# Weight preparation on estimated time: rests between a transfer and its first reader counted in estimated microseconds instead of scheduler ticks, an earlier and partly VectorE-made second gate chunk

## The chip, the cores and the metric

One core of one Trainium2 chip runs the whole program in one launch. The metric is the device time of an execution in microseconds (us). TensorE is called PE, VectorE DVE, ScalarE ACT, GpSimd POOL, and SP is the engine whose queue issues most of the DMA transfers.

## The reference, cut to what matters

```python
x = A_x                                     # (1, 2048, 576), f32
xn = _layernorm(x)
qkv = (xn @ wqkv).reshape(B, S, 3, 32, 18)  # 32 heads of 18
p = softmax(einsum("bhqd,bhkd->bhqk", q, k) * 18 ** -0.5)
s = einsum("bhqk,bhkd->bhqd", p, v) ... @ wo
h = gelu(xn @ w_gate) * (xn @ w_up)         # 576 -> 4608
g = silu(h @ w_down)                        # 4608 -> 576
return x + s * g
```

## The kernel before, in words

Every f32 matrix product is made of f16 products: a matrix is scaled by a power of two and split into a high and a low f16 half, and three of the four products of halves are added up in PSUM. The normed input is split once (`XHT`, `XL`). The weights are split while the program runs, in *chunks*: the projection groups `j0` to `j4` (seven heads' query and key columns each), the value weights `v`, eighteen gate/up/down chunks `c0` to `c17` of 256 hidden columns each, and `wo`. The order is v, j1, c0, c1, j2, c2, c3, j3, c4, c5, j4, c6, ... c17, wo.

`prep` (L195) makes the list of pieces by which one chunk is prepared. The **load** issues the DMAs of the raw weights: two for the gate, two for the up columns (L215, L219), and for a `c` chunk one for the rows of `w_down` (L227). There is one raw buffer and one down buffer, so a load waits on SP until POOL has read the chunk before to its end. Then DVE takes the **absolute maximum** of the five 128-row tiles (L234) and of the two down tiles (L239), and of these (`par`, L248, L251); a column of 128 maxima goes out to DRAM (L260, tile `mxd`), comes back spread over all partitions (`spread`, L275, tile `mb`), and DVE reduces it (`top`, L281, tile `mg`) and makes scale factors of it (L286 to L298, tiles `E` and `s`). ACT then writes the five **high halves** (L316), and POOL the five **low halves** in two instructions each (L323, L324); `fin` marks the chunk as ready. The halves of the down rows follow, and `dfin`.

These pieces lie in one queue, `bg`. The program that records the instructions calls `subtick` once per step of its main loops; each call is a **tick**, with a budget of time on ACT, DVE and, through `"T"`, on POOL. A tick records up to three pieces (six in a tick that closes a pair of gate products) while the budget lasts. An empty piece `(None, None)` ends the tick: a **rest** of n such pieces makes the queue wait n ticks. Rests stand ahead of the load (`lead`), between the load and the first maximum, between `par` and `spread`, between `spread` and `top`, and ahead of the high halves. A tick has no fixed length on the chip. In the first attention loop (pair 0, L1440 on) two ticks go with each pair of score tiles, in the main loop (L1560 on) one tick goes with each score tile and its share of other work.

Each engine runs its own instructions in the order of recording, so a piece recorded early stands ahead of all that its engine records later, and where it has to wait, the rest of that engine's work waits too. The other DVE work: the maximum of each tile of scores (`PM`, L1235), which frees the PSUM buffer that PE needs two score tiles later; a one-element copy `touch` (L422), after which PE begins the second half of a pair of gate products (`Pair`, L454); the sums `osb` of the products with V (L1331, L1333) after each burst of them (L1325), `y` (L764), and the small steps at the end of a head pair (`max_end`, L1245 to L1254).

The norm of an attention output goes through DRAM as well, in steps that are put off by a number of ticks (`norm`, `chained`): `sd`, `oc` (L1361), the reciprocal (L1364), `rd` (L1368), the spread denominators `obr` (L1372, 256 KB), and four ticks later the product on DVE (L1375). These DMAs, the loads of Q, K and V tiles, the stores of projected Q and K (L520) and the chunk loads all go through SP, in one order.

A chunk must be ready when its first product is recorded (`unit_w`, `until`). `start_prep` (L964) queues chunk i + 1 and i + 2 when unit i begins.

Of the kernel before, what the change touches and what calls it, by code (L numbers as in the profile page):

```python
# [33 lines left out]
FIRST = {"A": 0.75, "V": 0.75, "T": 1.3}  # L34
FREE = {"A": 4.0, "V": 4.0, "T": 1.3}
# [6 lines left out]
class Deferred:  # L42
# [4 lines left out]
    def __init__(self):  # L47
        self.now = 0
        self.items = []
        self.n = 0  # L50
        self.room = {}
        self.pool = 0.0

    def at(self, when, fn, cost=None):
        self.items.append((max(when, self.now + 1), self.n, fn, cost))
        self.n += 1
# [13 lines left out]
    def advance(self, room):  # L70
        self.now += 1
        self.room = dict(room)
        self.pool = max(0.0, self.pool - room["T"])
        while True:
            due = [i for i in self.items if i[0] <= self.now and self.fits(i[3])]
            if not due:
                return
            i = min(due, key=lambda i: i[:2])
            self.items.remove(i)
            self.spend(i[3])  # L80
            i[2]()


def on_act(t=0.7):
    return {"A": t}


def on_dve(t=0.7):
    return {"V": t}


def on_pool(t):
    return {"G": t}
# [3 lines left out]
def kernel(ctx: ExitStack, tc: tile.TileContext, x, wqkv, wo, w_gate, w_up, w_down, out):  # L97
# [11 lines left out]
    class Stage:  # L109

        def __init__(self):
            self.sb = self.pt = None
# [18 lines left out]
    defer = Deferred()  # L131
    bg = deque()
# [5 lines left out]
            self.open = open  # L138


    def subtick(room=FREE, most=3):
        defer.advance(room)
        n = 0
        while bg and n < most:
            if isinstance(bg[0], Gate):
                if not bg[0].open():
                    return
                bg.popleft()
                continue
            cost, fn = bg[0]  # L150
            if not defer.fits(cost):
                return
            defer.spend(cost)
            bg.popleft()
            n += 1
            if fn is None:
                return
            fn()
# [33 lines left out]
    class W:  # L192
        pass

    def prep(name, parts, n, down=None, urgent=False, free=None, dfree=None, lead=1, slow=0):  # L195


        w = W()
        w.ready = w.dready = False
        w.n = n  # L200
        pieces = []
        gap = 0 if urgent else 1
        q = nc.sync
        npart = len(parts)

# [106 lines left out]
        def split_hi(t):  # L312
            if t == 0:
                w.hi = wp.tile([P, 5, 2, n], F16, tag="whi", name=f"whi_{name}")
                w.lo = wp.tile([P, 5, 2, n], F16, tag="wlo", name=f"wlo_{name}")
            nc.scalar.activation(w.hi[:, t], w.raw[:, t], AF.Copy, scale=w.s[:, 0:1])  # L316

        def low(lo, raw, sc, hi):

            if urgent:  # L320
                nc.vector.scalar_tensor_tensor(lo, raw, sc, hi, op0=ALU.mult, op1=ALU.subtract)
            else:
                nc.gpsimd.tensor_scalar(raw, raw, sc, None, op0=ALU.mult)  # L323
                nc.gpsimd.tensor_tensor(lo, raw, hi, op=ALU.subtract)  # L324

        def split_lo(t):
            low(w.lo[:, t], w.raw[:, t], w.s[:, 0:1], w.hi[:, t])

        def dsplit_hi(t):
            if t == 0:  # L330
# [13 lines left out]
        def add(fn, cost=None):  # L344
            pieces.append((cost, fn))

        def rest(n):
            for _ in range(n * gap):
                pieces.append((None, None))

        act, dve = on_act(), on_dve()
        low_cost = dve if urgent else on_pool(2.75)
        pieces += [(None, None)] * (lead * gap)
        add(load)
        rest(5 + slow)
        for t in range(5):
            add(lambda t=t: amax(t), dve)
        if down is not None:
# [2 lines left out]
        add(par, dve)  # L361
        if urgent:
            add(par2)
        rest(3)
        add(spread)
        rest(4)
        add(top, on_dve(0.4))
        for fn in (power, floor, inverse):
            add(fn, on_dve(0.2))
        rest(1)  # L370
        if free is not None:
            pieces.append(Gate(free))
        for t in range(5):
            add(lambda t=t: split_hi(t), act)
            if t:
                add(lambda t=t: split_lo(t - 1), low_cost)
        add(lambda: split_lo(4), low_cost)
        if down is not None:
            add(units, on_dve(0.2))
            add(back, on_dve(0.3))  # L380
# [181 lines left out]
    def spec_j(j):  # L562
        n = DH * len(heads_of(j))
        return f"j{j}", [(wqkv, 126 * j), (wqkv, D + 126 * j)], n
# [400 lines left out]
    def start_prep(i):  # L965
        if i < len(order) and i not in preps:
            kind, spec = order[i]
            w, pieces = prep(
                *spec, free=lambda: done_units[0] >= i - 1,
                dfree=lambda: kind[1] < 2 or dndone[kind[1] - 2] == NT,  # L970
                lead=8 if i == 3 else 1, slow=2 if i == 2 else 0,
            )
            preps[i] = w
            bg.extend(pieces)
            if kind == "wo":
                bg.extend(begin_wo(w))
# [77 lines left out]

    def fills(n, amt):
        for _ in range(n):
            subtick()
            fill(amt)


    w0, p0 = prep(*spec_j(0), urgent=True)
# [82 lines left out]
    with tc.manual_schedule():  # L1144
        for t in range(4):
            load_x(t, 1, nc.scalar)
        p0[0][1]()
        for t in range(4, NT, 4):
            load_x(t, 4, nc.sync)
        nc.vector.memset(epst, EPS)  # L1150
        pw = [f for _, f in p0[1:] if f is not None]
        s0, s1 = ln_stats(0, 2), ln_stats(2, 2)
        for f in s0:
            f()
        ln_norm(0)
        ln_norm(1)
        for f in s1[:3] + pw[:5]:
            f()
        ln_tr(0)
        ln_out(0)  # L1160
        for f in pw[5:6] + s1[3:7] + pw[6:12] + s1[7:]:
            f()
        ln_norm(2)
        pw[12]()
        ln_tr(1)
        ln_out(1)
        for f in pw[13:]:
            f()
        lnq = deque()
        for t in range(4, NT, 4):  # L1170
            lnq.extend(ln_stats(t, 4))
        for _ in range(12):
            lnq.popleft()()
        for it in range(2, NT + 2):
            g, i = divmod(it, 4)
            if 2 < it < NT:
                ln_norm(it)
            if g < 3:
                for _ in range((0, 0, 0, 5)[it] if it < 4 else (5, 4, 4, 4)[i]):
                    if lnq:  # L1180
                        lnq.popleft()()
            if it == 5:
                open_j(w0, 0)
            if it == 5:
                preps[0], pieces = prep(*order[0][1], urgent=True)
                pv0 = deque(f for _, f in pieces if f is not None)
                pv0.popleft()()
            for _ in range(V_PLAN.get(it, 0)):
                pv0.popleft()()
            if it == 2:  # L1190
                proj_fine(0)
            if it > 2:
                if it - 1 < NT:
                    ln_tr(it - 1)
                if it - 2 > 1:
                    ln_out(it - 2)
                subtick()
                proj_fine(it - 2)
        while pv0:
            pv0.popleft()()  # L1200
        start_prep(1)
        start_prep(2)
        for _ in range(3):
            subtick()
# [226 lines left out]
    filler[0] = unit_v(preps[0])  # L1431
    load_qk(0)
    fills(9, 2.0)
    k = 0
    while k < 64:
# [23 lines left out]
    for k in range(5):  # L1459
        if k in (0, 1, 3):  # L1460
            steps[k - k // 3]()
        g_run(14)
        if k:
            qk1(1, next(items))
        subtick(FIRST)
    assert mdone.get(0)

    def last_gen():
# [93 lines left out]
    for p in range(NPAIR - 1):  # L1562
        if p not in VT:
            load_v(p)
        for i in range(4 * NT):
# [22 lines left out]
            step = plan.popleft() if plan else None  # L1588
            late = False
# [9 lines left out]
            if d and not behind:  # L1599
                if dn is None:  # L1600
                    dn = DownPair()
                late = dn.run()
            if gs.closed:
                gs.closed = False
                if late:
                    dn.evac()
                    dn = None
                subtick({"A": 2.2, "V": 1.4 if late else 2.2, "T": 0.7 + 0.86 * len(pend) + 0.73 * d}, 6)
                flush(("ma", "mb") if d else ("md", "ma"))
                summed = not d  # L1610
            else:
                subtick({"A": 0.75, "V": 0.0 if late or step is not None and step[2] < 1.45 and len(bg) < 70 else 0.75, "T": 2.0 if step is None else 0.45 + step[2]})
                if late:
                    dn.evac()
                    dn = None
                g_run(7 if step is None else step[1])
                if behind:
                    dn = DownPair()
                    dn.run()
# [20 lines left out]
    for i in range(4 * NT):  # L1640
# [17 lines left out]
        if phase >= 2:  # L1658
            nphase = 0
            n = next((k + 1 for k, u in enumerate(pend) if u[2] == NT - 1), len(pend))  # L1660
# [61 lines left out]
```

## Time and profile before

| what | value |
| --- | --- |
| median of 3 runs | 2635.53 us (2624.99 to 2636.22) |
| the profiled execution | 2634.51 us |
| its span, from the first to the last instruction | 2632.7 us |
| mean granted PE clock | 0.989 |
| busy of the span | PE 96%, DVE 73%, ACT 63%, POOL 57% |

A row of the timeline reads: start, length, engine, line, operation, output<-inputs, shapes, count, and in brackets how long the engine sat idle before it and what ended that. A row of SP is the issue of a DMA, not its transfer. A row of the table of windows reads: stretch, its length, busy time and count for PE, for PE's weight loads, DVE, ACT and POOL, then the granted PE clock, the busy share of the DMA engines, and GB/s.

### The profile page before, as it was taken

How to read it: one execution, taken by the hardware profiler on the slowest of the kernel's cores; microseconds unless marked ns; L12 is line 12 of the kernel's file. 1: busy time of each engine (PE TensorE's matmuls, PEld its weight loads, DVE VectorE, ACT ScalarE, POOL GpSimd, SP SyncE). 2: the span in 40 equal slices, each digit the busy share in tenths (PEclk: the TensorE clock that was granted, in tenths of full speed). 3: DMA queues.
4: the chain of work that ended last, by engine and by line, in shares of the span. 5: the costliest groups of instructions: out<-in, count | busy, mean ns of one | idle time of the engine just before them, and what ended most of it. 6: DMA issues, size and time to landing. Idle time of an engine off the chain costs nothing.

```text
span 2632.7 us, 59553 instructions
## 1 busy us (share of the span) xinstructions
PE 2534.8 (96%) x25220; PEld 1317.2 (50%) x25220; DVE 1927.1 (73%) x2712; ACT 1664.6 (63%) x2083; POOL 1492.3 (57%) x1422
## 2 busy tenths in 40 slices
PE   6889999899999999999999999999999999999898
PEld 5554545345545454454544555455455554555344
DVE  7576778777777778777877777777777777777444
ACT  5225666666767666767666676677666666766563
POOL 4237653575527544758475675756566666747301
PEclk9999999999999999999999999999999999999999
DMA  4430022202030012112011111202010111100123
GB/s 144 138 99 13 16 58 61 49 18 57 21 88 19 26 38 63 29 39 54 12 36 28 37 26 38 56 10 56 10 49 15 35 27 39 49 9 10 35 77 118
DMA packets 133640, 118.61 MB, mean 45 GB/s; under 512 B 60160, under 2 KB 112792, under 8 KB 133372
## 3 DMA queue, kind: packets, MB, share of 16 engines
q1 hardware_dynamic: 127740, 103.02, 14.8%
q0 software_dynamic: 3072, 8.90, 1.0%
q8 instruction: 197, 3.23, 0.5%
q10 hardware_dynamic: 2560, 2.89, 0.3%
q14 instruction: 71, 0.58, 0.1%
HBM read 84.89 MB, written 29.61 MB: 43 GB/s over the span
## 4 chain that ended last, share of the span: by engine, by line
PE 80%; DVE 9%; ACT 4%; DMA 3%; issue 2%; POOL 2%; SPq 1%; ACTq 0%; DVEq 0%; POOLq 0%
PE mb_t L454 15%; PE ma_t L454 15%; PE md_t L744 14%; PE md_t L1325 8%; PE s L1284 8%; PE s L1232 7%; PE ma_t L1325 6%; DVE PM L1235 3%; ACT P L1290 1%; PE pv L1306 1%; PE mc_t L473 1%; PE mb_t L473 1%; PE ma_t L473 1%; DVE m_c L234 1%; DMA obr<-rd 1%
## 5 line engine op out<-in xcount | busy, mean ns | idle before, releaser
L1235 DVE TENSOR_REDUCE PM<-s 128x2 f32<-128x1024 f32 x1024 | 1250.9, 1224 | 338.9 <-PE s L1232 330.4
L1290 ACT ACTIVATE P<-s,etab 128x1024 f32<-128x1024 f32 x896 | 997.9, 1114 | 620.4 <-PE s L1284 608.0
L454 PE MATMUL ma_t<-XHT,whi_c 64*128 64x512 f16 x1440 | 544.5, 378 | 13.2 <-ACT gs L619 7.8
L454 PE MATMUL mb_t<-XHT,whi_c 64*128 64x512 f16 x1440 | 544.4, 378 | 13.3 <-DVE touch L422 10.1
L454 PE MATMUL ma_t<-XHT,wlo_c 64*128 64x512 f16 x1296 | 489.5, 378 | 0.0
L454 PE MATMUL ma_t<-XL,whi_c 64*128 64x512 f16 x1152 | 435.5, 378 | 0.0
L454 PE MATMUL mb_t<-XHT,wlo_c 64*128 64x512 f16 x1152 | 435.4, 378 | 0.0
L454 PE MATMUL mb_t<-XL,whi_c 64*128 64x512 f16 x1152 | 435.2, 378 | 0.0
L1232 PE MATMUL s<-KT,QT 54*128 54x512 f16 x2048 | 399.3, 379 | 16.5 <-DVE PM L1235 13.8
L1284 PE MATMUL s<-QT,KT 56*128 56x512 f16 x2048 | 402.2, 381 | 8.1 <-ACT P L1290 2.5
L454 PEld LDWEIGHTS <-whi_c 64*128 64x128 f16 x5184 | 277.5, 94 | 256.0 <-issue 44.6
L744 PE MATMUL md_t<-dhi_c,hhi 64*128 64x288 f16 x2216 | 327.8, 283 | 2.8 <-DVE touch L422 1.3
L744 PE MATMUL md_t<-dhi_c,hlo 64*128 64x288 f16 x2216 | 327.3, 282 | 0.0
L744 PE MATMUL md_t<-dlo_c,hhi 64*128 64x288 f16 x2216 | 326.9, 282 | 0.0
L655 POOL TENSOR_SCALAR tw<-tw 128x512 f32<-128x512 f32 x144 | 91.0, 632 | 411.4 <-ACT tw L648 411.1
L744 PEld LDWEIGHTS <-hhi 64*128 64x128 f16 x4432 | 236.8, 94 | 133.3 <-issue 17.2
L677 POOL TENSOR_TENSOR hlo<-gv,hhi 128x512 f16<-128x512 f32 x144 | 168.4, 1169 | 217.4 <-ACT hhi L670 208.5
L1325 PE MATMUL md_t<-P,VT 128*32 128x512 f32 x2368 | 274.9, 596 | 0.4 <-DVE y L764 0.3
L1284 PEld LDWEIGHTS <-KT 56*128 56x128 f16 x2048 | 125.2, 94 | 268.4 <-issue 179.3
L642 POOL TENSOR_TENSOR tw<-gs 128x512 f32<-128x512 f32 x144 | 150.4, 1044 | 166.6 <-ACT gs L619 166.0
L764 DVE SCALAR_TENSOR_TENSOR y<-md_t,c_c,y 128x576 f32<-128x576 f32 x261 | 210.4, 806 | 1.0 <-PE md_t L744 1.0
L454 PEld LDWEIGHTS <-wlo_c 64*128 64x128 f16 x2592 | 139.9, 94 | 121.9 <-issue 3.0
(270 smaller groups left out, 4054.9 us busy)
## 6 DMA issues: line engine op xcount, KB each, us to landing
draw_c<-in_B_w_down SPq DMA_DIRECT2D x18, 576.0 KB
raw_c<-in_B_w_gate SPq DMA_DIRECT2D x18, 512.0 KB
raw_c<-in_B_w_up SPq DMA_DIRECT2D x18, 512.0 KB
obr<-rd SPq DMA_DIRECT2D x30, 256.0 KB
KT<-KD SPq DMA_DIRECT2D x32, 224.0 KB
QT<-QD SPq DMA_DIRECT2D x32, 216.0 KB
VS<-vst POOLq DMA_DIRECT2D x16, 304.0 KB, 3.6
VT<-VS SPq DMA_DIRECT2D x16, 304.0 KB
```

What stands on the lines that cost most here:

```text
L454: nc.tensor.matmul(o, lw, xx, start=self.stage == 0 and self.k == 0, stop=self.stage == 1 and self.k == self.slots - 1, skip_group_check=True,
L473: nc.tensor.matmul(o, xx(t), ww[:, t, i, :], start=(k == 0), stop=False)
L642: gp.tensor_tensor(st["t"], st["g"], st["g"], op=ALU.mult)
L655: gp.tensor_scalar(st["t"], st["t"], 1.0, 1.0, op0=ALU.mult, op1=ALU.add)
L677: gp.tensor_tensor(hs.lo[:, ft], st["v"], hs.hi[:, ft], op=ALU.subtract)
L744: nc.tensor.matmul(self.t.t[:, hf, 0:288], a[r, ft, sl], b[r, ft, 288 * hf:288 * hf + 288], start=self.stage == 0 and k == 0, stop=self.st ...
L764: nc.vector.scalar_tensor_tensor(yy, y, w.c, yy, op0=ALU.mult, op1=ALU.add)
L1232: nc.tensor.matmul(s1[:, h], QT[p][r, P * qt:P * qt + P], KT[p][r, 512 * kb:512 * kb + 512], start=True, stop=True)
L1235: nc.vector.tensor_reduce(PM[p][:, :, qt, kb:kb + 1], s1, op=ALU.max, axis=AX.X)
L1284: nc.tensor.matmul(s2[:, h], KT[p][r, P * kt:P * kt + P], QT[p][r, 512 * qb:512 * qb + 512], start=True, stop=True)
L1290: nc.scalar.activation(pt, s2, AF.Exp, scale=ETAB[j0])
L1325: nc.tensor.matmul(t.t[qd:qd + 32, :], VT[p][:, c0:c0 + 32], pt[:, h], start=kt == k0, stop=kt == k1, skip_group_check=True,)
```

## The change

A rest is now an object `Rest` with a span in estimated microseconds. The scheduler adds up the `"T"` of all ticks as its time, and a rest is over at the first tick that begins at least that span after the tick in which it was reached; it no longer ends the tick for what follows it. The `"T"` of the nine steps after `load_qk(0)` (`fills`) is 2.0 instead of 1.3, and that of the five steps ahead of the main loop 3.2. The second gate chunk `c1` (i == 3) had a lead of eight ticks and has one of two times 1.9 us; two of its five low halves (tiles 1 and 3) go to DVE in one instruction each. In ticks that had no DVE budget there is now 0.25.

```diff
     def advance(self, room):
+        self.time += room["T"]
...
+    class Rest:
+        def over(self):
+            if self.start is None:
+                self.start = defer.time
+            return defer.time - self.start >= self.span
...
+            if isinstance(bg[0], Rest):
+                if not bg[0].over():
                     return
                 bg.popleft()
                 continue
...
-            if urgent:
+            if urgent or vec:
                 nc.vector.scalar_tensor_tensor(lo, raw, sc, hi, op0=ALU.mult, op1=ALU.subtract)
...
-        pieces += [(None, None)] * (lead * gap)
+        rest(1.9 * lead)
         add(load)
-        rest(5 + slow)
+        rest(13.0)
...
-        rest(3)
+        rest(4.0)
         add(spread)
-        rest(4)
+        rest(6.5)
         add(top, on_dve(0.4))
...
-        rest(1)
+        rest(0.5)
...
-                lead=8 if i == 3 else 1, slow=2 if i == 2 else 0,
+                lead=2 if i == 3 else 1, vec=(1, 3) if i == 3 else (),
...
-            subtick()
+            subtick(dict(FREE, T=amt))
...
-        subtick(FIRST)
+        subtick(dict(FIRST, T=3.2))
...
-  "V": 0.0 if late or step is not None and step[2] < 1.45 and len(bg) < 70 else 0.75,
+  "V": 0.25 if late or step is not None and step[2] < 1.45 and len(bg) < 70 else 0.75,
```

PE's instructions stand in the same order in both kernels; the order on DVE, ACT, POOL and SP differs. Line numbers of the changed kernel are 18 or 19 higher in the pieces of `prep` and the loops.

On DVE, at the start of the first attention loop, stands the reduction of the spread maxima of j1 (`mg_j`, `E_j`) among the maxima of score tiles (`PM`). Before:

```order
L1235 TENSOR_REDUCE PM_1080<-s_0_2_1304 128x2
L1235 TENSOR_REDUCE PM_1080<-s_0_3_1308 128x2
L281 TENSOR_REDUCE mg_j_1312<-mb_j_1256 128x1
L286 TENSOR_SCALAR E_j_1314<-mg_j_1312 128x1
L1235 TENSOR_REDUCE PM_1080<-s_0_4_1336 128x2
L1235 TENSOR_REDUCE PM_1080<-s_0_5_1340 128x2
```

and now, at the same place:

```order
L1253 TENSOR_REDUCE PM_1080<-s_0_4_1332 128x2
L1253 TENSOR_REDUCE PM_1080<-s_0_5_1336 128x2
L1253 TENSOR_REDUCE PM_1080<-s_0_6_1358 128x2
L1253 TENSOR_REDUCE PM_1080<-s_0_7_1362 128x2
L1253 TENSOR_REDUCE PM_1080<-s_0_8_1386 128x2
L1253 TENSOR_REDUCE PM_1080<-s_0_9_1390 128x2
L299 TENSOR_REDUCE mg_j_1395<-mb_j_1310 128x1
L304 TENSOR_SCALAR E_j_1397<-mg_j_1395 128x1
```

The reduction moved behind six more score tiles. On SP, the load of c1 stands among the stores of j1's projections (`KD`, `QD`, four groups of six). Before:

```order
L520 DMA QD_1882<-evl_0_2_2171 7x18x512
L215 DMA raw_c_2203<-in_B_w_gate 128x4x256
L219 DMA raw_c_2203<-in_B_w_gate 128x1x256
L215 DMA raw_c_2203<-in_B_w_up 128x4x256
L219 DMA raw_c_2203<-in_B_w_up 128x1x256
L227 DMA draw_c_2208<-in_B_w_down 128x2x576
L520 DMA KD_1883<-evh_1_3_2260 7x18x512
L520 DMA KD_1883<-evl_1_3_2262 7x18x512
```

and now:

```order
L538 DMA QD_1869<-evl_0_3_2255 7x18x512
L233 DMA raw_c_2346<-in_B_w_gate 128x4x256
L237 DMA raw_c_2346<-in_B_w_gate 128x1x256
L233 DMA raw_c_2346<-in_B_w_up 128x4x256
L237 DMA raw_c_2346<-in_B_w_up 128x1x256
L245 DMA draw_c_2351<-in_B_w_down 128x2x576
L1242 DMA VT_2443<-VS 128x16x38
L835 DMA OHL<-zeros 36x512 x8
L278 DMA mxd_c_2653<-mx_c_2650 128x2
```

The load moved behind the last group of stores, and c1's column of maxima (`mxd`) behind the zero stores. Its first maximum moved with it on DVE: it stood ahead of the first `touch` of c0's products and stands now behind the first three. Also on SP, the load of c3 and the norm's `rd` and `obr`; before the load stood between them:

```order
L1368 DMA rd_0_6121<-oc_0_5957 128x16
L215 DMA raw_c_6123<-in_B_w_gate 128x4x256
L219 DMA raw_c_6123<-in_B_w_gate 128x1x256
L215 DMA raw_c_6123<-in_B_w_up 128x4x256
L219 DMA raw_c_6123<-in_B_w_up 128x1x256
L227 DMA draw_c_6128<-in_B_w_down 128x2x576
L1372 DMA obr_0_6181<-rd_0_6121 128x1x512
```

Now it stands behind `obr`. At the load of c8, c12 and c17 it is the other way round: the load stood ahead of `rd` (c8) or behind `obr` (c12, c17), and stands now between them, as here at c8:

```order
L1386 DMA rd_1_15500<-oc_1_15343 128x16
L233 DMA raw_c_15536<-in_B_w_gate 128x4x256
L237 DMA raw_c_15536<-in_B_w_gate 128x1x256
L233 DMA raw_c_15536<-in_B_w_up 128x4x256
L237 DMA raw_c_15536<-in_B_w_up 128x1x256
L245 DMA draw_c_15541<-in_B_w_down 128x2x576
L1390 DMA obr_1_15563<-rd_1_15500 128x1x512
```

The small load of j4 comes to stand so as well; the other chunks have no load between the two, before or now.

More of the change, by code (lines that the diff above doesn't have):

```diff
@@ L52, in __init__ @@
         self.pool = 0.0
+        self.time = 0.0
     def at(self, when, fn, cost=None):
@@ L138, in __init__ @@
             self.open = open
+    class Rest:
+        def __init__(self, span):
+            self.span, self.start = span, None
+        def over(self):
+            if self.start is None:
+                self.start = defer.time
+            return defer.time - self.start >= self.span
     def subtick(room=FREE, most=3):
@@ L146, in subtick @@
                 if not bg[0].open():
+                    return
+                bg.popleft()
+                continue
+            if isinstance(bg[0], Rest):
+                if not bg[0].over():
                     return
@@ L193, with prep @@
         pass
-    def prep(name, parts, n, down=None, urgent=False, free=None, dfree=None, lead=1, slow=0):
+    def prep(name, parts, n, down=None, urgent=False, free=None, dfree=None, lead=1, vec=()):
         w = W()
@@ L201, in prep @@
         pieces = []
-        gap = 0 if urgent else 1
         q = nc.sync
@@ L316, in split_hi, with low @@
             nc.scalar.activation(w.hi[:, t], w.raw[:, t], AF.Copy, scale=w.s[:, 0:1])
-        def low(lo, raw, sc, hi):
-            if urgent:
+        def low(lo, raw, sc, hi, vec=False):
+            if urgent or vec:
                 nc.vector.scalar_tensor_tensor(lo, raw, sc, hi, op0=ALU.mult, op1=ALU.subtract)
@@ L326, in split_lo @@
         def split_lo(t):
-            low(w.lo[:, t], w.raw[:, t], w.s[:, 0:1], w.hi[:, t])
+            low(w.lo[:, t], w.raw[:, t], w.s[:, 0:1], w.hi[:, t], t in vec)
         def dsplit_hi(t):
@@ L345, in add, with rest @@
             pieces.append((cost, fn))
-        def rest(n):
-            for _ in range(n * gap):
-                pieces.append((None, None))
+        def rest(span):
+            if not urgent:
+                pieces.append(Rest(span))
         act, dve = on_act(), on_dve()
-        low_cost = dve if urgent else on_pool(2.75)
-        pieces += [(None, None)] * (lead * gap)
+        low_cost = [dve if urgent or t in vec else on_pool(2.75) for t in range(5)]
+        rest(1.9 * lead)
         add(load)
-        rest(5 + slow)
+        rest(13.0)
         for t in range(5):
@@ L375, in prep @@
             if t:
-                add(lambda t=t: split_lo(t - 1), low_cost)
-        add(lambda: split_lo(4), low_cost)
+                add(lambda t=t: split_lo(t - 1), low_cost[t - 1])
+        add(lambda: split_lo(4), low_cost[4])
         if down is not None:
@@ L1150 @@
         nc.vector.memset(epst, EPS)
-        pw = [f for _, f in p0[1:] if f is not None]
+        pw = [f for _, f in p0[1:]]
         s0, s1 = ln_stats(0, 2), ln_stats(2, 2)
@@ L1185 @@
                 preps[0], pieces = prep(*order[0][1], urgent=True)
-                pv0 = deque(f for _, f in pieces if f is not None)
+                pv0 = deque(f for _, f in pieces)
                 pv0.popleft()()
@@ L1611 @@
             else:
-                subtick({"A": 0.75, "V": 0.0 if late or step is not None and step[2] < 1.45 and len(bg) < 70 else 0.75, "T": 2.0 if step is None else 0.45 + step[2]})
+                subtick({"A": 0.75, "V": 0.25 if late or step is not None and step[2] < 1.45 and len(bg) < 70 else 0.75, "T": 2.0 if step is None else 0.45 + step[2]})
                 if late:
```

## The prediction

> **What bounds the kernel now.** I read the page's busy shares first, then the chain that ended last.
>
> ```profile
> PE 2534.8 (96%) x25220; PEld 1317.2 (50%) x25220; DVE 1927.1 (73%) x2712; ACT 1664.6 (63%) x2083; POOL 1492.3 (57%) x1422
> PE 80%; DVE 9%; ACT 4%; DMA 3%; issue 2%; POOL 2%; SPq 1%; ACTq 0%; DVEq 0%; POOLq 0%
> ```
>
> PE is busy 96% of the span and holds 80% of the chain. Its instructions and their order don't change, so the time can only change by PE's idle time, some 98 us of 2632.7, and by its clock. I went through the timeline of PE for idle time ahead of an instruction (in brackets) and kept what is over 2 us between the projections' start and the last head pair:
>
> ```profile
> 98.40 0.61 PE L1232 MATMUL s<-KT,QT 54*128 54x512 f16 x2 [6.05 <-DVE PM L1235]
> 188.94 0.58 PE L454 MATMUL mb_t<-XHT,whi_c 64*128 64x512 f16 x1 [6.62 <-DVE touch L422]
> 475.64 0.37 PE L454 MATMUL mb_t<-XHT,whi_c 64*128 64x512 f16 x1 [2.88 <-DVE touch L422]
> 511.60 0.27 PE L1254 MATMUL md_t<-ident,rmc 128*64 128x128 f16 x1 [3.07 <-DVE osb L1333]
> 665.37 0.22 PE L1254 MATMUL md_t<-ident,rmc 128*64 128x128 f16 x1 [2.83 <-DVE osb L1333]
> 760.68 0.37 PE L454 MATMUL ma_t<-XHT,whi_c 64*128 64x512 f16 x1 [2.37 <-DVE osb L1331]
> 1049.91 0.45 PE L1232 MATMUL s<-KT,QT 54*128 54x512 f16 x2 [2.05 <-DVE PM L1235]
> ```
>
> I call them A to G. All seven wait for DVE, though DVE is idle a quarter of the time: it is held up, or it has a train of work at the wrong moment. Five of them cost more than the gap. The table of windows, laid on the stretches of lower clock, has PE busy in its second pair of numbers and the granted clock third from the end:
>
> ```profile
> 94.39:104.63 10.24, 5.71 (x24) 2.56 (x23) 5.35 (x9) 2.28 (x6) 3.84 (x7) 0.50 0.38 118
> 186.55:193.37 6.82, 4.43 (x22) 1.90 (x23) 4.86 (x7) 0.00 (x0) 0.00 (x0) 0.50 0.35 119
> 476.68:480.09 3.41, 3.41 (x19) 1.46 (x16) 2.42 (x4) 1.63 (x2) 0.00 (x0) 0.50 0.00 0
> 510.81:517.64 6.83, 6.04 (x39) 2.79 (x40) 2.88 (x5) 3.19 (x5) 2.88 (x4) 0.50 0.02 4
> 1050.12:1053.53 3.41, 3.41 (x18) 1.49 (x16) 2.03 (x3) 0.51 (x1) 0.00 (x0) 0.50 0.24 70
> ```
>
> Work at half clock takes twice as long, so half of PE's busy time there is lost: 2.9 us after A, 2.2 after B, 1.7 after C, 3.0 after D, 1.7 after G. E and F have none.
>
> **The change part by part: what it takes away.**
>
> A. DVE sat 6.93 us at the reduction of j1's spread maxima, with the score maxima behind it:
>
> ```profile
> 78.28 0.36 SPq L260 DMA_DIRECT2D mxd_j<-mx_j  x1
> 92.13 0.35 SPq L275 DMA_DIRECT2D mb_j<-mxd_j  x1
> 96.74 0.29 DVE L281 TENSOR_REDUCE mg_j<-mb_j 128x1 f32<-128x128 f32 x1 [6.93 <-DMA mb_j<-mxd_j]
> 104.68 2.36 DVE L1235 TENSOR_REDUCE PM<-s 128x2 f32<-128x1024 f32 x2 [2.49 <-PE s L1232]
> 107.22 2.36 DVE L1235 TENSOR_REDUCE PM<-s 128x2 f32<-128x1024 f32 x2 [0.18 <-PE s L1232]
> ```
>
> The transfers keep their places behind the Q and K loads, so the maxima still land at 96.7. The reduction now follows six more score tiles, three pairs at 2.5 us (104.68 to 107.22): it is reached at 89.8 + 7.6 = 97.4 instead of 89.8, and waits for nothing. Saved: 6.05 and 2.9, 9.0 us. What is late next is ACT's copy of a value tile, whose buffer came free around 92, at most 0.5.
>
> B. DVE reached c1's first maximum before the load had landed, with c0's `touch` behind it:
>
> ```profile
> 176.66 0.42 SPq L215 DMA_DIRECT2D raw_c<-in_B_w_gate  x1
> 186.42 0.69 DVE L234 TENSOR_REDUCE m_c<-raw_c 128x1 f32<-128x512 f32 x1 [4.64 <-DMA raw_c<-in_B_w_up]
> 167.79 0.37 PE L454 MATMUL mb_t<-XHT,whi_j 64*126 64x512 f16 x1 [0.64 <-DVE touch L422]
> ```
>
> The load takes 9.8 us. Now three `touch` copies stand ahead of the first maximum, so PE waits for this `touch` as long as for the one of the stage before, 0.6 us (at 167.79). Saved: 6.0 of the 6.62, and 2.2 of clock, 8.2 us. The load's five DMAs moved past six stores, which only makes these stores earlier; c1's `mxd` behind the zero stores has about 15 us until its reduction. c0's pieces, though, are now recorded 78 to 124 matmuls later. Their cover:
>
> ```profile
> 162.46 1.16 POOL L324 TENSOR_TENSOR wlo_c<-raw_c,whi_c 128x512 f16<-128x512 f32 x1
> 150.00:175.00 25.00, 23.39 (x212) 18.58 (x208) 20.41 (x28) 6.08 (x11) 19.16 (x14) 1.00 0.27 83
> ```
>
> The last low half was done at 163.6, and PE was through the half pair that reads it at 182.3 (188.94 less 6.62). 124 matmuls at 25 us per 212 are 14.6 us, so about 4 us of cover stay. I count nothing; if the cover were gone, PE would wait here, up to 2.7 us per missing low half (the third rival).
>
> C. c3's load stood between `rd` and `obr`:
>
> ```profile
> 456.80 0.33 SPq L1368 DMA_DIRECT2D rd<-oc  x1
> 457.23 0.39 SPq L215 DMA_DIRECT2D raw_c<-in_B_w_gate  x1
> 461.27 2.96 SPq L227 DMA_DIRECT2D draw_c<-in_B_w_down  x1
> 464.34 0.67 SPq L1372 DMA_DIRECT2D obr<-rd  x1
> 474.58 0.95 DVE L1375 TENSOR_TENSOR osb<-osb,obr 128x512 f32<-128x512 f32 x1 [2.50 <-DMA obr<-rd]
> ```
>
> SP came to `obr` 7.5 us after `rd`, and the denominators landed behind the load, 17.7 us after `rd`. The load now follows `obr`: saved 2.88 and 1.7, 4.6 us. c2's low halves end up recorded right ahead of c2's first product; POOL has no other work there (j2's products need none), and takes them as ACT delivers, so I count nothing; bounds 0 and one low half, 2.7.
>
> D to G are trains on DVE:
>
> ```profile
> 508.93 0.80 DVE L292 TENSOR_SCALAR E_c<-E_c 128x2 f32<-128x2 f32 x1
> 510.03 0.92 DVE L298 TENSOR_SCALAR s_c<-s_c 128x2 f32<-128x2 f32 x1
> 510.86 0.68 DVE L1333 TENSOR_TENSOR osb<-md_t,osb 128x512 f32<-128x512 f32 x1
> 663.32 1.40 DVE L239 TENSOR_REDUCE m_c<-draw_c 128x1 f32<-128x576 f32 x2
> 758.03 1.40 DVE L239 TENSOR_REDUCE m_c<-draw_c 128x1 f32<-128x576 f32 x2
> 1046.27 1.86 DVE L234 TENSOR_REDUCE m_c<-raw_c 128x1 f32<-128x512 f32 x3
> ```
>
> PE's burst had ended at 508.5 (511.60 less 3.07), and it needs the sum `osb` of it. By the new order c3's scale factors, or c4's maxima at E, no longer stand ahead of it: DVE could take it at once, 0.7 us and two hand-overs, say 0.9. D saves 2.2 and 3.0, E 1.9. At F and G, c5's and c7's maxima stood in one train with the low halves of j3's and j4's last stores, and now come later. That takes 2.1 us of work out at F (the row and one maximum of 0.7), 1.9 at G, with its clock 3.6. Together **A to G give 9.0 + 8.2 + 4.6 + 5.2 + 1.9 + 2.1 + 3.6 = 34.6 us.**
>
> [...]
>
> **What it adds.** c8, c12 and c17 now have their load where c3's was. At c8:
>
> ```profile
> 1131.09 0.34 SPq L1368 DMA_DIRECT2D rd<-oc  x1
> 1145.49 0.83 DVE L1375 TENSOR_TENSOR osb<-osb,obr 128x512 f32<-128x512 f32 x1
> 1148.02 0.69 DVE L1333 TENSOR_TENSOR osb<-md_t,osb 128x512 f32<-128x512 f32 x1 [0.51 <-PE md_t L1325]
> ```
>
> If `obr` lands 17.7 us after `rd`, at 1148.8, DVE waits 3.3 us at the product and ends it at 1149.6. Here PE has a burst to run meanwhile, whose sum DVE took at 1148.02, so it is late by 1.6. I take 1.6 at each of the three, 4.8 us. Bounds: nothing, and what C shows, the 3.3 with its 0.4 more on PE and the longest clock loss of the main loop, 3.0: 6.7 each, 20 in all. j4's load is small and has no down rows: nothing, same upper bound for one.
>
> Other trains form: by the order, with the durations of such rows, DVE has 37 places in the main loop with over 2.3 us of work between two score maxima, before and now; in the old kernel four of them cost over 2 us. The worst new ones (c2's maxima beside j2's stores; c4's beside two sums) resemble old ones without a gap; I take 1.5 us, bounds 0 and two like G, 7.5.
>
> The two low halves on DVE have no row of their size with these operands; nearest:
>
> ```profile
> 17.10 3.13 DVE L321 SCALAR_TENSOR_TENSOR wlo_j<-raw_j,s_j,whi_j 128x252 f16<-128x252 f32 x5 [1.15 <-ACT whi_j L316]
> 250.00:275.00 25.00, 24.99 (x266) 12.81 (x262) 18.86 (x23) 18.11 (x22) 18.34 (x17) 1.00 0.01 2
> ```
>
> 0.6 us for half the columns, so some 1.2 each, in a stretch where DVE is idle for a quarter and PE for 0.01 us: nothing, bounds 0 and 2.4. The DVE budget of 0.25 lets instructions of some 0.2 us into tight ticks, each after a score maximum: nothing, at most 0.9 as at E.
>
> **Sum.** 34.6 less 4.8, 1.5 and ACT's 0.5 is 27.8: 2634.5 (the profiled execution; span and 1.8 around it) becomes 2606.7. The median of the runs stands 1.0 above that execution, so I predict **2608**.
>
> **The rivals.** A change below 0.5%, 13 us, can't be told from none here.
>
> - *The norm's denominators cost in full.* c8, c12 and c17 behave like C: 20 for 4.8, so 2623 at worst, 2618 with the clock lost at one of them only. For it: the same three instructions in the same order. Against: the burst that PE has at hand. 15%.
> - *The clock is luck.* The half clock after C, D and G belongs to this execution; then 6.4 us of the gain isn't there: 2614. For it: the run of 2624.99, and E and F without it. 10%.
> - *Stalls re-form.* The rests do what they say, but as many trains as before fall somewhere else, and c0's low halves lose their cover: C to G (17.4) return, A and B stay less 2.7, and the three loads cost 4.8: 2635.5 - 17.2 + 2.7 + 4.8 = 2626, within 0.5%. For it: 37 places in both kernels. 13%.
> - *Slower: trains in the long ticks.* A rest counted in time ends most often in the longest tick, the one that closes a pair and takes six pieces; there the new kernel records three maxima together some 20 times, the old one some 16, and all of `top` to `s` in one tick for most chunks. If over nine of these stop PE at G's 3.8 us, they outweigh the gain; with fourteen, 53 us, the time is 2608 + 53 = 2661. Against: of the old ones G alone did, and only beside a store's low half. 7%.
>
> The forecast, 2598 to 2616, holds 55%. Below 2600 it would need all gains and no loss: 2635.5 - 34.6 = 2601, and PE's small waits for DVE gone too. The range of 2596 to 2625 takes in the second-worst bound and most of the third rival. Faster by over 0.5% (below 2622): 80%; within 0.5%: 13%; slower: 7%.
>
> **What would show it.** Right: no gap over 1 us on PE near 92 and 182 and the clock at 1.00 there; no DVE wait for `mb_j` or `raw_c`; about 70 us of PE idle in all. At the load of c8, c12 and c17 a DVE wait for `obr` of about 3 us and a PE gap of about 1.6. Wrong: a PE gap ahead of c0's or c2's first products for a low half; POOL's `wlo_c` as what ended it; gaps of 2 us and half clock at trains that the old kernel didn't have.

## The result and the profile after

| kernel | median, us | lowest to highest | runs |
| --- | --- | --- | --- |
| before | 2631.97 | 2624.99 to 2636.22 | 10 |
| after | 2622.05 | 2620.83 to 2622.95 | 10 |

The ratio is 0.9963 (95% interval 0.9953 to 0.9973): the change is worth 9.9 us, 0.37%. The forecast was 2608, a gain of 27.5. The profiled execution of the changed kernel took 2621.11 us, 13.4 less than that of before. Its busy shares and its chain:

```profile
PE 2526.9 (96%) x25220; PEld 1315.2 (50%) x25220; DVE 1930.7 (74%) x2714; ACT 1662.9 (63%) x2083; POOL 1487.4 (57%) x1418
PE 77%; DVE 10%; ACT 4%; DMA 3%; POOL 3%; issue 3%; SPq 0%; ACTq 0%; DVEq 0%; POOLq 0%
```

They look much as before, and the page doesn't tell where 13.4 us went. PE's idle time in the span fell from 97.9 us to 92.4, not to the 70 that the prediction named as a sign. The timeline shows the places, because PE runs the same instructions in the same order in both kernels: the start of the n-th matmul after, less that of the n-th before, is the time won up to there, and its steps show the places.

| matmuls | time before, us | place | forecast, us | measured, us |
| --- | --- | --- | --- | --- |
| 720-780 | 81-89 | first Q and K tiles | 0 | +10.2 |
| 780-840 | 89-106 | A | -9.0 | -9.3 |
| 1380-1440 | 179-195 | B | -8.2 | -8.1 |
| 2940-3060 | 347-360 | j2 | 0 | +7.9 |
| 4200-4260 | 472-483 | C | -4.6 | -4.7 |
| 4440-4500 | 506-518 | D | -5.2 | -5.0 |
| 5940-6000 | 656-666 | E | -1.9 | -1.9 |
| 6900-6960 | 755-764 | F | -2.1 | -1.9 |
| 9780-9840 | 1047-1058 | G | -3.6 | -3.2 |
| all others | | added waits, trains | +6.8 | +2.5 |
| sum | | | -27.8 | -13.4 |

The terms are rounded. All seven gaps went by about what the working gave them, and two new places of 10.2 and 7.9 us came. A's step stands here right behind a late Q tile; e10 below has the same 9.3 with Q in time. The two new gaps are the only idle times of PE over 2 us left between the projections and the last head pair; their rows in PE's timeline, and from the table of windows the stretches of half clock behind them (PE's busy time is the second number, the clock the third from the end):

```profile
93.00 1.03 PE L1250 MATMUL s<-KT,QT 54*128 54x512 f16 x3 [7.90 <-DMA QT<-QD]
351.21 0.42 PE L762 MATMUL md_t<-dhi_c,hhi 64*128 64x288 f16 x2 [5.10 <-DVE osb L1351]
```

```profile
87.06:97.30 10.24, 4.30 (x18) 2.24 (x18) 2.36 (x2) 0.41 (x1) 0.16 (x1) 0.50 0.19 46
349.89:356.72 6.83, 5.51 (x38) 3.12 (x39) 4.49 (x9) 2.01 (x3) 1.57 (x2) 0.50 0.11 19
```

In the second stretch, at 0.50, a pair of gate products (64x512) starts every 0.43 us (355.33 to 356.61), and behind it, at 1.00, every 0.21 us (357.54 to 358.18). So half of the busy time is lost, 2.2 and 2.8 us, and the places cost 10.1 and 7.9.

**The first.** SP's timeline before has the last of j1's four load DMAs (630 KB in all) ahead of the last three stores of projected K, and the Q and K loads behind these:

```profile
67.27 0.58 SPq L219 DMA_DIRECT2D raw_j<-in_A_wqkv  x1
...
70.13 0.74 SPq L520 DMA_DIRECT2D KD<-evh  x1
...
77.18 0.28 SPq L1216 DMA_DIRECT2D QT<-QD  x1
```

After, from the last of these stores on:

```profile
69.06 0.74 SPq L538 DMA_DIRECT2D KD<-evh  x1
69.85 0.45 SPq L233 DMA_DIRECT2D raw_j<-in_A_wqkv  x1
...
74.99 2.26 SPq L1233 DMA_DIRECT2D KT<-KD  x1
77.55 0.27 SPq L1234 DMA_DIRECT2D QT<-QD  x1
...
83.13 0.35 SPq L278 DMA_DIRECT2D mxd_j<-mx_j  x1
93.32 0.35 SPq L293 DMA_DIRECT2D mb_j<-mxd_j  x1
```

The load's lead of 1.9 us ends one tick later than one tick did, and it is now issued behind the stores, right ahead of the Q and K loads. SP's issues take up to 2.26 us each there, but the first Q load is issued only 0.4 us later than before: it is the landing that comes late, near 93. On DVE this shows as:

```profile
80.66 1.38 DVE L252 TENSOR_REDUCE m_j<-raw_j 128x1 f32<-128x252 f32 x4 [11.80 <-DMA raw_j<-in_A_wqkv]
93.64 2.36 DVE L1253 TENSOR_REDUCE PM<-s 128x2 f32<-128x1024 f32 x2 [10.54 <-PE s L1250]
108.07 0.28 DVE L299 TENSOR_REDUCE mg_j<-mb_j 128x1 f32<-128x128 f32 x1
```

The maxima landed later too, and `mg_j` doesn't wait for them: the long rest did what it should, and PE's wait moved ahead of it.

**The second.** SP and DVE at j2:

```profile
330.73 0.32 SPq L278 DMA_DIRECT2D mxd_j<-mx_j  x1
...
333.11 0.26 SPq L1411 DMA_DIRECT2D OHL<-onh  x1
...
346.18 0.26 SPq L1411 DMA_DIRECT2D OHL<-onl  x1
346.49 0.34 SPq L293 DMA_DIRECT2D mb_j<-mxd_j  x1
```

```profile
349.51 0.29 DVE L299 TENSOR_REDUCE mg_j<-mb_j 128x1 f32<-128x128 f32 x1 [6.11 <-DMA mb_j<-mxd_j]
350.48 0.68 DVE L1351 TENSOR_TENSOR osb<-md_t,osb 128x512 f32<-128x512 f32 x1
```

The spread load `mb_j`, issued at 326.35 before, now stands behind the Q and K loads and eight stores of the norm, which went out between 333.1 and 346.2. DVE stood at `mg_j` for 6.11 us with the sum `osb` behind it, and PE needs that sum's buffer. What SP itself waited for there (who waited for what, us in total, times, longest):

```profile
SPq L278 <- DVE mx_j L266: 25.3, 1, 25.3
SPq L1411 <- DMA mxd_j<-mx_j: 3.1, 1, 3.1
SPq L1411 <- DMA KT<-KD: 3.0, 2, 2.2
SPq L1411 <- DMA QT<-QD: 1.9, 2, 1.0
```

SP stood at `mxd_j` until j2's late maxima were done, so the Q and K loads behind it went out late as well (from 331.10 on). Of the stores (L1411) one waited for DVE (3.0 us), one for ACT (0.4), and five for `mxd_j` and the Q and K loads to land, 8.0 us together.

**What was to be lost at c8, c12 and c17.** DVE at c8, and then at c12 (c17 is like it):

```profile
1133.71 1.20 DVE L1393 TENSOR_TENSOR osb<-osb,obr 128x512 f32<-128x512 f32 x1 [1.61 <-DMA obr<-rd]
1134.83 0.68 DVE L1351 TENSOR_TENSOR osb<-md_t,osb 128x512 f32<-128x512 f32 x1
```

```profile
1579.57 0.73 DVE L1393 TENSOR_TENSOR osb<-osb,obr 128x512 f32<-128x512 f32 x1 [2.09 <-DMA obr<-rd]
```

DVE does wait for `obr`, 1.6 to 2.1 us for the 3.3 worked out, but at c8 PE's burst, from 1130.84 on and 3.64 long, ends at 1134.5, and the sum starts at 1134.8. PE's starts lose 0.3 us there, and 0.5 at each of c12 and c17.

### The profile page after: what moved, and what is told of

It reads as the page before. It is cut to its first block, busy times and chain, and to the rows that moved or that the text cites. A ratio compares the mean times of both kernels' runs of the same rounds, so it can differ in the third digit from the quotient of the medians.

```text
span 2619.3 us, 59543 instructions
## 1 busy us (share of the span) xinstructions
PE 2526.9 (96%) x25220; PEld 1315.2 (50%) x25220; DVE 1930.7 (74%) x2714; ACT 1662.9 (63%) x2083; POOL 1487.4 (57%) x1418
## 4 chain that ended last, share of the span: by engine, by line
PE 77%; DVE 10%; ACT 4%; DMA 3%; POOL 3%; issue 3%; SPq 0%; ACTq 0%; DVEq 0%; POOLq 0%
PE mb_t L472 15%; PE ma_t L472 14%; PE md_t L762 14%; PE s L1302 8%; PE md_t L1343 7%; PE s L1250 7%; PE ma_t L1343 5%; DVE PM L1253 3%; ACT P L1308 1%; DMA obr<-rd 1%; PE pv L1324 1%; DMA QT<-QD 1%; PE mc_t L491 1%; DVE m_c L252 1%; DVE osb L1351 1%
```

## The experiments

The theory was that the two transfers explain the miss: each gap is made by one DMA's place in SP's order, and undoing that place gives its time back. The main rival was that stalls re-form wherever the pieces fall. The runs were made in three groups beside 49 more runs of the kernel before (medians of 2628.98 to 2630.69), and the ratios are to these. The kernel before had 2631.97 beside the changed kernel, so a difference to "after" is uncertain by some 2 us; each trace is one execution.

### e1: j1's load ahead of the stores again

```diff
-                lead=2 if i == 3 else 1, vec=(1, 3) if i == 3 else (),
+                lead=2 if i == 3 else 0.5 if i == 1 else 1, vec=(1, 3) if i == 3 else (),
...
-        rest(6.5)
+        rest(8.0 if name == "j1" else 6.5)
```

> The changed kernel with j1's load issued one tick earlier, ahead of the last three KD stores as in the kernel before, and j1's reduction left behind ten score maxima. Theory (transfers): the 7.90 us wait for QT and the 10.24 us of half clock behind it come from j1's load standing right ahead of the Q and K loads; both go, Q lands near 85 us, and PE is 9 to 10 us earlier from its 840th product on: 2612 to 2613. Rival 1 (the Q and K loads wait for the last KD stores anyway): the gap stays, 2622. Rival 2 (stalls re-form): the 7.9 us go, but PE waits as long for the reduction of j1 near 92 or for c0's pieces: 2618 to 2622.

2612.41 us (ratio 0.9928, 0.9916 to 0.9941), 9.6 less than after. In the trace 7.8 of it is won at matmuls 720 to 780 and 1.1 at j2. Q lands some 5.7 us sooner, though not quite in time:

```profile
87.34 0.60 PE L1250 MATMUL s<-KT,QT 54*128 54x512 f16 x3 [2.06 <-DMA QT<-QD]
```

The load's place was the cause of the larger part of the gap; this one has no half clock behind it. All twelve traces agree: PE waits 7.9 to 9.0 us for the Q tile in the four with the load right ahead of the Q and K loads (after, e2, e6, e8), and 0 to 3.1 us in the seven with it ahead of the stores. The twelfth is e7, where the load stands behind them.

### e2: j2's spread load ahead of the norm's stores

```diff
-        rest(13.0)
+        rest(5.0 if name == "j2" else 13.0)
...
-        rest(6.5)
+        rest(14.5 if name == "j2" else 6.5)
```

> The changed kernel with j2's maxima and its spread load moved 8 us of estimated time earlier and its reduction left where it was; the spread load then is issued ahead of the Q and K loads and of the eight output stores. Theory (transfers): DVE's 6.11 us wait for mb_j, PE's gap of 5.10 at 346 and the 6.83 us of half clock go; about 7.9 us: 2614. Rival (the output stores or the sum osb themselves hold PE there): gap of 3 us or more stays, 2619 to 2622. j1's gap of 7.90 at 85 stays in either.

2614.32 us (ratio 0.9934, 0.9922 to 0.9946), 7.7 less; the trace has 8.0 at matmuls 2940 to 3060 and nothing else. SP issues the load 25 us sooner, and DVE's reduction and the sum behind it take their turn without the wait:

```profile
321.56 0.32 SPq L293 DMA_DIRECT2D mb_j<-mxd_j  x1
```

```profile
343.54 0.28 DVE L299 TENSOR_REDUCE mg_j<-mb_j 128x1 f32<-128x128 f32 x1
...
345.21 0.69 DVE L1351 TENSOR_TENSOR osb<-md_t,osb 128x512 f32<-128x512 f32 x1 [0.64 <-PE md_t L1343]
```

On DVE only j2's maxima changed places here, on SP only `mb`, and `mxd` went out at 314.27 instead of 330.73. So j2's late maxima and spread load are shown as the cause. Which of the two places counts, `mb` behind the stores or `mxd` ahead of the Q and K loads, this edit doesn't tell apart: in e2 no store waits for a landing any more, and the last is issued at 338.62.

### e3: both

The edits of e1 and e2 together.

> Both edits. Theory (transfers): the two are independent and add up, 9.5 and 7.9 from 2622: 2604 to 2605, with no PE gap over 1.5 us between the projections and the last attention pair, and the clock at 1.00 there throughout. Rival (stalls re-form): a new gap of over 2 us appears elsewhere and 2609 or more is left.

2607.58 us (ratio 0.9909, 0.9895 to 0.9922): 14.5 less than after and beyond both kernels. It is 3 short of the expected sum, all of it at the Q tile, where 2.17 us of wait are left and fell so that 3.41 us of half clock followed. No other gap of over 1.4 us is left between the projections and the last head pair: here nothing re-formed.

### e4: step A alone, in the kernel before

```diff
-        rest(4)
+        rest(9 if name == "j1" else 4)
...
-                lead=8 if i == 3 else 1, slow=2 if i == 2 else 0,
+                lead=3 if i == 3 else 1, slow=2 if i == 2 else 0,
```

> The kernel before with j1's reduction alone moved behind ten score maxima (its rest nine ticks, and c1's lead shortened so that SP's order stays as it was). This is step A by itself. If the step was right as worked out, the 6.05 us gap at 92.35 and its half clock go and no other takes their place: 9 us, 2623 against 2632. Rival (PE is held there by something else as well, such as ACT's value copies or c0's later pieces): 3 us or less, with a new gap between 92 and 190. The gaps B to G stay.

2630.61 us against 2630.69 (ratio 0.9997, 0.9988 to 1.0006): nothing. In the trace A's 9.3 us are won at matmuls 780 to 840, and by matmul 1440 all but 1.2 is given back: 2.5 of it at the Q tile (with SP's order unchanged) and 4.3 at two `touch` copies, which stand behind c0's scale factors and products on DVE (c0's pieces come after j1's in the one queue):

```profile
147.57 0.37 PE L454 MATMUL mb_t<-XHT,whi_j 64*126 64x512 f16 x1 [1.35 <-DVE touch L422]
...
164.01 0.37 PE L454 MATMUL mb_t<-XHT,whi_j 64*126 64x512 f16 x1 [1.96 <-DVE touch L422]
```

The rival was right here: A alone is worth nothing, and in this trace the pieces behind it give back what it won. How much of the 9.3 is the edit's stays open, since e5 has 8.7 of it there without the edit.

### e5: step B alone, in the kernel before

```diff
-                lead=8 if i == 3 else 1, slow=2 if i == 2 else 0,
+                lead=18 if i == 3 else 1, slow=2 if i == 2 else 0,
```

> The kernel before with c1's load alone put off (lead of 18 ticks for 8), so that it stands behind the last KD and QD stores. This is step B by itself. If B was right as worked out and needs none of the other parts, PE's gap of 6.62 us at 182 and the half clock behind it go: 8 us, 2623 against 2631, and gaps A and D to G stay. Rival (as with step A alone, what stands behind in the one queue of pieces comes late in its turn: c1's low halves or j2's): a new gap between 195 and 350, 2627 or more.

2625.98 us against 2629.81 (ratio 0.9988, 0.9980 to 0.9997). B's gap is gone, 8.1 us as worked out, and 5.2 of it comes back one stage later, since the maxima kept their distance of five ticks to the load, and DVE again stood at the first of them:

```profile
189.75 0.69 DVE L234 TENSOR_REDUCE m_c<-raw_c 128x1 f32<-128x512 f32 x1 [3.50 <-DMA raw_c<-in_B_w_up]
```

In the changed kernel, where the rest is 13 us of estimated time, that maximum came at 201.12 without a wait: the later load alone isn't enough for B. The longer rest alone was not run. This run also holds a second look at A and C with the order of before. At j1 `mg_j` waited

```profile
93.98 0.28 DVE L281 TENSOR_REDUCE mg_j<-mb_j 128x1 f32<-128x128 f32 x1 [0.40 <-DMA mb_j<-mxd_j]
```

0.40 us, not 6.93, behind a Q tile that was 2.27 late; over matmuls 720 to 840 it was 4.6 us faster than the execution shown of before, with nothing changed there. At C the gap was 1.34 here and 1.36 in e4, not 2.88, without half clock, 3.2 us less. The one execution from which the prediction took A and C had them large.

### e6: all of c1's low halves on POOL

```diff
-                lead=2 if i == 3 else 1, vec=(1, 3) if i == 3 else (),
+                lead=2 if i == 3 else 1, vec=(),
```

> The changed kernel with all five low halves of c1 on POOL again. The halves themselves cost or save nothing in any theory (0 to 2.4 us). But all later pieces fall elsewhere: j2's spread load is issued ahead of the norm's output stores, and no load stands between rd and obr at j4 and c8. Theory (transfers): j2's gap of 5.10 at 346 and its half clock go, about 7.9 us, and none comes in their place: 2614, no further change from j4 and c8, where the load cost nothing. Rival (stalls re-form wherever the pieces fall): 2619 or more, with a gap of over 2 us at another chunk. The gap at 85 stays in either.

2627.82 us against 2629.81 (ratio 0.9991, 0.9983 to 1.0000), 5.8 slower than after. j2's gap went, 8.0 us. But 8.6 came at matmuls 2220 to 2280, where PE waited for ACT and ACT for POOL:

```profile
281.87 0.61 PE L1302 MATMUL s<-QT,KT 56*128 56x512 f16 x2 [6.15 <-ACT P L1308]
```

```profile
278.86 0.63 ACT L688 ACTIVATE hhi<-gv 128x512 f16<-128x512 f32 x1 [3.64 <-POOL gv L674]
```

and E, F and G stand in the trace again with the lengths they had before (2.83, 2.37 and 2.06 us). Here the rival holds: with the halves elsewhere, all later pieces fall into other ticks.

### e7: both edits, with j1's load behind the Q and K loads

```diff
-                lead=2 if i == 3 else 0.5 if i == 1 else 1, vec=(1, 3) if i == 3 else (),
+                lead=2 if i == 3 else 2.1 if i == 1 else 1, vec=(1, 3) if i == 3 else (),
```

> The kernel of both edits, with j1's load behind the Q and K loads in place of ahead of the last KD stores. Theory (transfers): it is the small load ahead of Q and K that makes the 2.1 us wait for QT that was left at 85, so this goes too, with its 1.7 us of clock where it has some: 2604 to 2605. Rival 1 (QT waits for the last KD stores): the 2.1 stays, 2607 to 2608. Rival 2: j1's maxima now land too late, and PE waits over 2 us behind DVE at j1's reduction or c0's scale factors: 2609 or more.

2613.83 us (ratio 0.9935, 0.9923 to 0.9948), 6.2 more than e3. The wait for the Q tile is gone in this trace. That the load made it, and not the stores, isn't shown, since it is also absent before and in e10, with the load ahead of both. And j1's maxima now land at 87, and DVE and PE wait there:

```profile
87.55 1.38 DVE L252 TENSOR_REDUCE m_j<-raw_j 128x1 f32<-128x252 f32 x4 [18.62 <-DMA raw_j<-in_A_wqkv]
```

```profile
90.96 0.39 PE L1250 MATMUL s<-KT,QT 54*128 54x512 f16 x2 [3.63 <-DVE PM L1253]
```

c0's pieces come late behind them, and a `touch` at 147 costs 2.2 with half clock. Rival 2 was right.

### e8 and e9: no DVE budget in tight ticks

```diff
-  "V": 0.25 if late or step is not None and step[2] < 1.45 and len(bg) < 70 else 0.75,
+  "V": 0.0 if late or step is not None and step[2] < 1.45 and len(bg) < 70 else 0.75,
```

e8 has this edit in the changed kernel, e9 in that of e3.

> The changed kernel with the DVE budget of 0.25 in tight ticks back at 0.0. By its order nothing changes at j1, c1 and j2, so both new gaps (7.90 at 85, 5.10 at 346) stay; c8's and j4's obr come ahead of the load. Theory (transfers): 2622 within 1 us, as the budget and the loads at j4 and c8 cost nothing. Rival (the small instructions in tight ticks cost score maxima their place): 2 to 5 us faster, 2617 to 2620.

> The kernel of both edits with the DVE budget of 0.25 in tight ticks at 0.0. Theory (budget): the small instructions in tight ticks cost PE about 1.2 us each at two places (near 245 and 470 here), and without the budget a wait of 2.4 us comes back near 490 (c3's maxima ahead of the sum osb, as with the budget at 0.0 alone): the two nearly cancel, 2606 to 2608, the same as with both edits. Rival (the 3.8 us that the budget alone was worth are a gain of their own): 2603 to 2605.

e8: 2618.23 us (ratio 0.9955, 0.9943 to 0.9967), 3.8 less than after; but by the ratios it is 2.1, with intervals that overlap, and by the traces 1.7, so this gain is unclear. e9: 2606.89 (ratio 0.9915, 0.9901 to 0.9928), the same as e3 within the spread. The budget costs 1.2 to 1.3 us at each of two places, where PE waits for a score maximum, and saves the wait D, which comes back without it (2.43 us for the sum `osb`, at 506.96 in e8).

In e8's trace 1.6 us was won at j2's gap, whose half clock was half as long, so with that gap gone little is left. In both runs `obr` stands ahead of c8's load, and no step over 0.6 us shows there.

### e10: one of c1's halves back on POOL

```diff
-                lead=2 if i == 3 else 0.5 if i == 1 else 1, vec=(1, 3) if i == 3 else (),
+                lead=2 if i == 3 else 0.5 if i == 1 else 1, vec=(3,) if i == 3 else (),
```

> The kernel of both edits with one of c1's two low halves (tile 1) back on POOL; by its order that is the only instruction that goes to another engine, no DMA moves, and on DVE three small rows change places. Theory (POOL): c1's late load has put its low halves into the stretch where POOL works off c0's first activations; with both on POOL the gap at 276 was 6.15 us, so one half more, 2.7 us of POOL, brings a PE gap of 2 to 3 us for an ACT result near 266, with half clock behind it if it falls into one window: 2610 to 2612. Rival (it was the changed places of the other pieces, not POOL's load): no gap, 2607 to 2608.

2606.35 us (ratio 0.9912, 0.9898 to 0.9925), the same as e3, and no gap near 266. The theory of POOL's load fell for one half; whether e6's gap comes from both halves or from the moved pieces stays open. In this profiled execution Q landed in time: 3.8 us won at matmuls 720 to 780 with SP's order unchanged, as in the execution shown of before. Against that one it has all seven steps, A's 9.3 among them, and is 33.4 us shorter.

## Why the prediction was wrong

**The step that failed** is A's sentence "The transfers keep their places behind the Q and K loads, so the maxima still land at 96.7", and the part "What it adds", which counted the loads that came to stand between `rd` and `obr` and no other transfer. In place of the first, j1's own load had moved three stores back, right ahead of the Q and K loads, for 10.2 us (e1: 9.6 back). In place of the second, j2's maxima had come late: SP stood at their column with the Q and K loads behind it, and the spread load came behind these and eight stores, five of which waited for the landings, for 7.9 us (e2: 7.7 back). Neither move is in the list of moved transfers under "The change". With both undone the time is 2607.58; this near match with 2608 is no proof of the forecast's sum, since its errors partly cancel there. The sum's start was off as well: 2635.53 was a median of three, and ten runs have 2631.97, so 3.6 us of the forecast gain lay in that start.

**A to G** were right in cause and size for the execution they were worked out from: 34.6 forecast, 34.1 measured. But e4 and e5 show that A and B don't stand alone, and that with the order unchanged A cost 4.6 us less in e5, and C 3.2 less in both, than in that execution. That execution took 2.5 us more than the median of before, and the profiled one of after 0.9 less than its median, which is how 9.9 us between the medians became 13.4; that A and C are the reason is likely, not shown.

**c8, c12 and c17** were mis-sized: 4.8 forecast, some 1.2 measured. `obr` was there 16.1 us after `rd` was issued at c8, not 17.7, and the burst covered most of the rest.

**The two halves on DVE** were rightly costed at nothing where they run, though they took 1.52 and 1.63 us and not some 1.2 each. Their effect is on the places of all later pieces (e6), which no duration shows.

**The rivals.** The first, denominators in full, gave 2618 to 2623; 2622 lies there, but by luck, as they cost only those 1.2 us. "Stalls re-form" named the right kind of event, at the wrong places: C to G didn't return, the two transfers did the harm. "The clock is luck" was right in that the half clock belonged to the execution: F's gap had none behind it before and has it in e5, G's the other way round (below). "Slower" through trains of maxima found nothing: outside the nine places the table's remainder is 2.5 us.

## What to carry to other kernels

When a planner's rests change, walk down the DMA queue of the new order, row by row: for each transfer that moved, by one place too, ask what now stands ahead of it (does it wait for an engine, or is it a large load?) and what right behind it (does an engine wait for that?). Where one engine's order is the same in two kernels, subtract the starts of its n-th instructions: the steps show every gain and loss with its place, before any theory. And look at a second execution before a gap's length enters a sum.

## What the runs showed of the hardware

These figures are read off the granted clock in the profiles of before, after and e5. In that of before the stretches at 0.50 behind A, B, C, D and G are 10.24, 6.82, 3.41, 6.83 and 3.41 us long, in that of after the two behind the new gaps 10.24 and 6.83; those left are one near 29 (3.41 in both), one near 2450 (10.24 before, 6.83 after), and one that the end cuts. So but for the last they all measure 3.41 us or two or three times that. Within each of the two executions their starts also lie whole multiples of that apart (A's at 94.39 and B's at 186.55: 27 times). Counted off from these starts, each execution falls into slices of 3.41 us, and PE's busy time can be taken for each. These are the slices that hold most of C, D, E, F and G in the execution of before, and behind them the next ones for E and F:

```profile
473.27:476.68 3.41, 1.04 (x10) 0.56 (x11) 2.10 (x4) 1.01 (x2) 2.20 (x2) 1.00 0.01 5
507.40:510.81 3.41, 1.13 (x12) 0.24 (x5) 3.24 (x6) 0.35 (x1) 3.24 (x4) 1.00 0.00 0
661.00:664.41 3.41, 1.54 (x16) 0.37 (x9) 3.41 (x5) 0.76 (x2) 3.24 (x4) 1.00 0.01 2
756.57:759.98 3.41, 1.74 (x16) 0.34 (x9) 3.41 (x7) 1.41 (x3) 0.00 (x0) 1.00 0.38 111
1046.71:1050.12 3.41, 1.36 (x13) 0.47 (x11) 3.15 (x5) 1.45 (x2) 0.00 (x0) 1.00 0.11 35
...
664.41:667.82 3.41, 2.36 (x26) 1.20 (x27) 2.28 (x4) 1.39 (x2) 0.55 (x2) 1.00 0.03 5
759.98:763.39 3.41, 2.71 (x26) 1.48 (x27) 2.45 (x6) 0.71 (x2) 0.00 (x0) 1.00 0.03 3
```

And in e5 those of E, F and G, with the next ones behind them:

```profile
652.13:655.54 3.41, 1.31 (x13) 0.56 (x14) 2.56 (x5) 0.51 (x2) 1.70 (x3) 1.00 0.00 0
747.71:751.12 3.41, 1.04 (x12) 0.43 (x10) 3.41 (x6) 1.27 (x2) 0.00 (x0) 1.00 0.26 77
1041.25:1044.66 3.41, 1.64 (x14) 0.76 (x14) 2.93 (x4) 0.86 (x1) 0.00 (x0) 1.00 0.08 20
...
655.54:658.95 3.41, 3.41 (x30) 1.95 (x28) 1.87 (x3) 1.99 (x2) 0.00 (x0) 0.50 0.04 10
751.12:754.53 3.41, 3.41 (x20) 1.50 (x16) 0.86 (x4) 0.37 (x1) 0.00 (x0) 0.50 0.12 24
1044.66:1048.07 3.41, 2.92 (x24) 1.18 (x23) 3.41 (x6) 2.23 (x2) 0.00 (x0) 1.00 0.19 55
```

Before, half clock followed the slices with 1.04, 1.13 and 1.36 us of busy PE, and not those with 1.54 and 1.74; in e5 it followed E's and F's (1.31 and 1.04) and not G's (1.64). F's gap of 2.37 us, before, lies in two slices, 1.67 us of idle PE in the first and 0.70 in the next; in e5 one slice holds 2.37 us of idle PE. Over the executions of before and after, from 25 us on, eleven slices at 1.00 had at most 1.45 us of busy PE, and all eleven were followed by 0.50; of six with 1.53 to 1.76 one was, and of those with more one, with 1.93. So in the one execution of before gaps of 2 to 3 us came with half clock behind them (C 2.88, G 2.05) and without (E 2.83, F 2.37). The five over 3 us in the rows of PE shown (A, B and D before, 7.90 and 5.10 after) all had it.
